# The third pair's decays and the last rows of batch 0 come by transfers instead of products, and the queue behind them is reordered

## The chip, the cores and the metric

The kernel runs on one core of a Trainium2 chip. The metric is the device time of one execution in microseconds (us), the median of several runs. Engines are named as in the profile: PE (matrix products), PEld (its weight loads), DVE (VectorE), ACT (ScalarE), POOL (GpSimd) and SP, whose queue issues nearly all transfers (DMAs).

## The reference

There are two stages. The first is a state space layer over 4 batches, 8 heads, 768 steps, 32 channels and 16 states, worked in chunks:

```python
log_a = np.log(np.clip(a, 1e-06, 1.0))
for c in range(nc):
    cum = np.cumsum(la, axis=-1)
    L = np.exp(cum[:, :, :, None] - cum[:, :, None, :]) * causal
    CB = np.einsum('bhin,bhjn->bhij', Cc, Bc)
    y_intra = np.einsum('bhij,bhjd->bhid', CB * L, xc)
    y_inter = np.einsum('bhin,bhnd->bhid', Cc, state) * decay_to_i[:, :, :, None]
    y[:, :, sl] = y_intra + y_inter
    state = decay_full[:, :, None, None] * state + np.sum(Bx, axis=2)
```

The second takes its output as 3072 tokens of 256 numbers through a layer of 2048:

```python
h = x @ w_in
g = h * (1.0 / (1.0 + np.exp(-1.702 * h)))
return (g @ w_out).astype(np.float32)
```

The two weights w_in and w_out are double precision in memory, and the kernel makes single precision of them itself.

## The kernel before

The tokens are worked in six groups of 512 (`g` = 0 to 5). A group has two *pairs* of chunks of 128 steps, so pair 0 and 1 belong to group 0, pair 2 and 3 (`PG` and `PG + 1`, here "the third and the fourth pair") to group 1. The change touches the stretch in which group 0 goes through both products while group 1's first stage is prepared, from about 22 to 82 us.

**The weights.** They come in ten pieces, 0 to 5 of w_in and 6 to 9 of w_out. `fetch(i)` issues two DMAs of a piece. `fields(i)` (L192, L195, on DVE) takes the words apart, `clamp(i)` (L203, L204, on ACT) bounds the exponent, `rounded(i)` (L208) adds the low word, and `join(i)` (L222, L228) writes the result into w_in or w_out; with `parts` 2 it does so in halves. `narrow(i)` does `rounded(i)`, `join(i)` and `fields(i + 1)`, and which of the last two comes first differs by piece. Raw words lie in four rotating buffers (`words`), which the spread decays share.

**Group 0's products.** `hidden(0, f)` for f = 0 to 15 makes one block h of the hidden layer by two products (L895), each a pair of records in the profile; ACT applies the nonlinearity (`silu`, L898). After them `project_all(0)` runs f = 0 to 15 again, with two products each into o0 and o1 (L992): f needs w_out's piece 6 + f / 4. Blocks h, the transposes `tp` and o0, o1 take turns in four PSUM banks.

**Group 1's preparation.** A pair's decay products within a chunk are a scan (`decay`, L405) over a, spread to all partitions; its end values scale B (`ends`, L464: Be). `spread(p)` brings the spread a by two DMAs of 256 KB from a scratch copy of a in DRAM, which `store_a` writes after a has been clipped. The third pair has another way: `pick_a` (ACT, L369) picks its rows, `fan_all` spreads them by products with ones (L415) into PSUM, and four scans (`decay_heads`, L453) follow. The decays since the start of a chunk (`since`) of batch 0's chunks 4 and 5 are likewise fanned out by products (L504, L533) and scanned in `since_fanned` (L546), while batch 1's come by one DMA (`spread_rows`, tile af), a clip (`clip_rows`, L483) and a scan (`decay_rows`, L496). `turn(p)` transposes B and C of a pair on PE (tp, L600), ACT copies them, and DVE multiplies C by `since` (CsT, L670). `score` (cb, L685), `gain` (A, L716), `keep_both`, `weigh` (L696) and `finish` (y, L825 and L839) complete the pair.

**What sets the order.** Every engine works in the order in which the program's lines are recorded; `in_order` keeps it. Dictionaries `in_hidden[0]` and `in_project[0]` say after which f of `hidden`, and before which f of `project_all`, a step is recorded:

```python
    at(in_hidden[0], 9, lambda: fan_all(PG))
    at(in_hidden[0], 9, since_fanned)
    at(in_project[0], 0, lambda: turn(PG), lambda: rounded(8),
       lambda: fields(9), lambda: join(8))
    at(in_project[0], 2, lambda: decay(PG + 1), lambda: clip_rows(1),
       lambda: decay_rows(1), lambda: turn(PG + 1))
    at(in_project[0], 9, lambda: score(pairs), lambda: gain(pairs), lambda: keep_both(pairs, True),
       lambda: weigh(PG), lambda: weigh(PG + 1))
    at(in_project[0], 15, lambda: finish(pairs))
```

From group 1 on the products take a form with seven instead of eight multiplications, for which DVE sums weights (`mix_in(n)`, L912: four sums for each of two blocks; `mix_w`) and values (`mix_y`, `mix_g`).

Of the kernel before, what the change touches and what calls it, by code (L numbers as in the profile page):

```python
# [16 lines left out]
P = 128  # L17
# [18 lines left out]
def kernel(  # L36
# [176 lines left out]
    NEXT = {1: (6,), 5: (9,)}  # L213
# [21 lines left out]
    def narrow(i):  # L235
        rounded(i)
        if i in (4, 5):
            join(i, 2)
        if i + 1 < len(PIECES):
            fields(i + 1)  # L240
        if i not in (4, 5):
            join(i)
# [23 lines left out]
    def spread_rows(b):  # L266
        raf[b] = raw.tile([P, NC, P], FP32, tag="af", name=f"af{b}", bufs=1)
        nc.sync.dma_start(out=raf[b].rearrange("p c s -> p (c s)"),
                          in_=a[b].unsqueeze(1).to_broadcast([NH, N, S]))

    def rows_a(t, queues):

        e = t.shape[1] * P
        for r in range(R):
            queues[r % len(queues)].dma_start(
                out=t[32 * r:32 * r + 32].rearrange("p c s -> p (c s)"),
                in_=a.rearrange("b h s -> (b h) s")[:, :e])
# [74 lines left out]
    starts, fans, flat = {}, {}, {}  # L352

    def clip(t, name):

        nc.vector.tensor_scalar(out=t, in0=t, scalar1=1e-6, scalar2=1.0,
                                op0=ALU.max, op1=ALU.min)
        starts[name] = const.tile([P, t.shape[1], 2], FP32, name=f"starts{name}")
        first = t.rearrange(by_chunk, s=2)[:, :, :, 0]
        nc.vector.tensor_copy(starts[name], first)  # L360
        nc.vector.memset(first, 0.0)

    def pick_a(p):

        b, c = divmod(2 * p, NC)
        X = ffn.tile([P, 2, DM], FP32, tag="ob", name=f"X{p}")
        X = fans[p] = X.rearrange("p k (q i) -> p k q i", q=Q)
        for q in range(Q):
            nc.scalar.activation(X[:, :, q], az[:, c:c + 2], AF.Copy, scale=pick[:, b, q:q + 1])  # L369

# [9 lines left out]
    pick = picker("pick", NB, 1, NH)  # L380
    whose = const.tile([32 * PG, 1 + PG, NH, N], FP32, name="whose")
    nc.gpsimd.memset(whose, 1.0)
    for i, n, head in ((0, 1, PG), (1, 2, PG), (0, 0, 1)):
        t = whose[32 * i:32 * i + 32, n:n + 1]
        nc.gpsimd.affine_select(out=t, in_=t, pattern=[[-1, 1], [-head, NH], [0, N]],
                                compare_op=ALU.is_equal, fill=0.0, base=-max(n - 1, 0),
                                channel_multiplier=1)
# [23 lines left out]
    def fan(p, r, ab):  # L411

        rows = slice(32 * r, 32 * r + 32)
        for i, side in enumerate(SIDES):
            nc.tensor.matmul(out=ab[side].rearrange("p (k q i) -> p k q i", k=2, q=Q),  # L415
                             lhsT=ones[rows, side], rhs=fans[p][rows][:, :, :, side],
                             start=True, stop=True, tile_position=(32 * r, H * i),
                             skip_group_check=True)

    def fan_all(p):  # L420

        ab = area(f"ab{p}")[:, :, :2 * Q * H]
        for r in range(R):
            fan(p, r, ab[:, r])
        fan_since()
        for r in range(R):
            decay_heads(p, r, ab[:, r])
        for k in range(2):
            ends(p, k)

# [15 lines left out]

    def decay_heads(p, r, ab):

        if r == 0:
            L = ssd.tile([P, R, 2 * Q * H], FP32, tag="L", name=f"L{p}", bufs=3)  # L450
            flat[p] = L
            Ls[p] = L.rearrange("p r (k q i) -> p k r q i", k=2, q=Q)
        nc.vector.tensor_tensor_scan(  # L453
            out=flat[p][:, r], data0=ab,
            data1=idents.rearrange("p h i -> p (h i)")[:, :2 * Q * H],
            initial=0.0, op0=ALU.mult, op1=ALU.add)
# [24 lines left out]
    def clip_rows(b):  # L481
        t = raf[b]
        nc.vector.tensor_scalar(out=t, in0=t, scalar1=1e-6, scalar2=1.0,  # L483
                                op0=ALU.max, op1=ALU.min)
        first = ssd.tile([P, NC, P], FP32, tag="first", name=f"first{b}", bufs=1)
        nc.gpsimd.memset(first, 0.0)
        f, t0 = (v.rearrange(by_chunk, s=2)[:, :, :, 0] for v in (first, t))
        nc.gpsimd.tensor_copy(f, t0)
        nc.gpsimd.memset(t0, 0.0)
        firsts[b] = first  # L490

    def decay_rows(b):

        t, first = raf.pop(b), firsts.pop(b)
        since[b] = ssd.tile([P, NC, P], FP32, tag="since", name=f"since{b}")
        nc.vector.tensor_tensor_scan(  # L496
            out=since[b].rearrange("p c s -> p (c s)"), data0=t.rearrange("p c s -> p (c s)"),
            data1=first.rearrange("p c s -> p (c s)"),
            initial=0.0, op0=ALU.mult, op1=ALU.add)

    def fan_rows(t, c0, c1, o):

        o = o[:, :(c1 - c0) * P]
        nc.tensor.matmul(out=o, lhsT=whose[:32, 0].rearrange("p h n -> p (h n)"),  # L504
                         rhs=t[:32, c0:c1].rearrange("p c s -> p (c s)"), start=True,
                         stop=True, tile_position=(0, 0), skip_group_check=True)
        return o

    def since_first():
# [3 lines left out]
        for p in range(PG):  # L513
            at = slice(32 * p, 32 * p + 32)
            nc.tensor.matmul(out=rows[p],
                             lhsT=whose[at, 1 + p].rearrange("p h n -> p (h n)"),
                             rhs=cum[at].rearrange("p k s -> p (k s)"), start=True, stop=True,
                             tile_position=(32 * p, 0), skip_group_check=True)
# [9 lines left out]

    def fan_since():
        o = bank("rows4")  # L530
        t = fanned["rows"] = fan_rows(az, CG, NC, o)
        f = fanned["starts"] = o[:, 2 * P:2 * P + 2 * (NC - CG)]
        nc.tensor.matmul(out=f, lhsT=whose[:32, 0].rearrange("p h n -> p (h n)"),  # L533
                         rhs=starts[1][:32, CG:].rearrange("p c s -> p (c s)"), start=True, stop=True,
                         tile_position=(0, 0), skip_group_check=True)

    fanned = {}

    def since_fanned():

        t, f = fanned["rows"], fanned["starts"]
        first = ssd.tile([P, NC, P], FP32, tag="first", name="first0", bufs=1)[:, CG:]
        nc.gpsimd.memset(first, 0.0)
        nc.vector.tensor_copy(first.rearrange(by_chunk, s=2)[:, :, :, 0],
                              f.rearrange("p (c s) -> p c s", s=2))
        nc.vector.tensor_tensor_scan(  # L546
            out=since[0][:, CG:].rearrange("p c s -> p (c s)"), data0=t,
            data1=first.rearrange("p c s -> p (c s)"), initial=0.0, op0=ALU.mult, op1=ALU.add)
# [340 lines left out]
    def hidden(g, f):  # L889
        j, i = divmod(f, 2)  # L890
        if i == 0:
            block(g, j)
        h = bank(f"h{g}_{f}")
        for k in range(NK):
            nc.tensor.matmul(out=h, lhsT=w_in[:, f, k], rhs=yT[g][:, k], start=(k == 0),  # L895
                             stop=(k == NK - 1), skip_group_check=True)

        nc.scalar.activation(gT[g, j][:, i], h, AF.Silu, scale=GELU_SCALE)  # L898
# [303 lines left out]
    rows_a(az, (nc.sync,))  # L1202
# [14 lines left out]
    load(PG)  # L1217
# [7 lines left out]
    def store_a():  # L1225
        clip(az, 1)
        for i, side in enumerate(SIDES):
            nc.sync.dma_start(out=scratch[:, i].rearrange("c r i -> r c i"), in_=az[:32, :, side])

    at(in_hidden[0], 5, store_a, lambda: fetch(7), lambda: fetch(8),  # L1230
       lambda: load(PG + 1))
    at(in_hidden[0], 8, lambda: pick_a(PG))
    at(in_hidden[0], 9, lambda: fan_all(PG))
    at(in_hidden[0], 9, since_fanned)
    for i, k, c in ((2, 1, 1), (3, 2, 2), (4, 4, 7), (5, 8, 11), (6, 11, 14), (7, 14, 15)):
        at(in_hidden[0], k, lambda i=i: narrow(i))
        at(in_hidden[0], c, lambda i=i: clamp(i + 1))
    at(in_hidden[0], 9, lambda: spread(PG + 1), lambda: spread_rows(1))
# [5 lines left out]
    at(in_project[0], 2, lambda: decay(PG + 1), lambda: clip_rows(1),  # L1244
       lambda: decay_rows(1), lambda: turn(PG + 1))
    at(in_project[0], 5, lambda: narrow(9))
    at(in_project[0], 9, lambda: score(pairs), lambda: gain(pairs), lambda: keep_both(pairs, True),
# [3 lines left out]
       lambda: load(n + 1, "x"), lambda: mix_in(2), lambda: mix_in(3),  # L1251
       lambda: turn_blocks(2), lambda: decay(n))
# [10 lines left out]
    at(after, "H1", lambda: turn_out(0, 0), lambda: turn_out(0, 1))  # L1263
# [62 lines left out]
    for j in range(2):  # L1326
        mix_g(1, j)
    run(1, "4.1 4.5 4.2 P P 4.6 P L P 4.7 P P P 4.D", seven(1, 0), L=more_loads)
# [121 lines left out]
```

## Time and profile before

| what | us |
|---|---|
| median of 3 runs | 349.3 (348.98 to 349.34) |
| profiled execution | 350.67 |
| its span, first to last instruction | 348.8 |
| PE busy | 341.6 |
| DVE busy | 254.6 |
| ACT busy | 155.0 |

The clock granted to PE was 1.0 throughout. The chain of work that ended last is PE for 90% of the span, DMA for 3%, DVE for 2%. A row of a timeline gives start, duration, engine, line, operation, tiles (out<-in) and, in brackets, the idle time of the engine before it and what ended it; rows of the chain give start, duration and what ran. Rows of SP are issues: their duration is the time that the queue took to accept them, not that of the transfer.

### The profile page before, as it was taken

How to read it: one execution, taken by the hardware profiler on the slowest of the kernel's cores; microseconds unless marked ns; L12 is line 12 of the kernel's file. 1: busy time of each engine (PE TensorE's matmuls, PEld its weight loads, DVE VectorE, ACT ScalarE, POOL GpSimd, SP SyncE). 2: the span in 40 equal slices, each digit the busy share in tenths (PEclk: the TensorE clock that was granted, in tenths of full speed). 3: DMA queues.
4: the chain of work that ended last, by engine and by line, in shares of the span. 5: the costliest groups of instructions: out<-in, count | busy, mean ns of one | idle time of the engine just before them, and what ended most of it. 6: DMA issues, size and time to landing. Idle time of an engine off the chain costs nothing.

```text
span 348.8 us, 8124 instructions
## 1 busy us (share of the span) xinstructions
PE 341.6 (98%) x3380; PEld 268.9 (77%) x3380; DVE 254.6 (73%) x481; ACT 155.0 (44%) x352; POOL 13.1 (4%) x42
## 2 busy tenths in 40 slices
PE   8989999999999999999999999999999999999996
PEld 6634444445688888888888888888888888899996
DVE  5889997999878999667997467788465654465463
ACT  4797585205453322654432554332564331554320
POOL 8300000100000100000000000000000000000000
PEclk9999999999999999999999999999999999999999
DMA  6599889624627200415704027400000300000301
GB/s 158 134 300 213 189 181 245 113 54 105 113 49 131 66 0 2 75 57 124 123 18 63 0 59 130 73 1 2 0 4 3 55 7 0 0 2 0 62 0 61
DMA packets 89980, 25.92 MB, mean 74 GB/s; under 512 B 73432, under 2 KB 87128, under 8 KB 89944
## 3 DMA queue, kind: packets, MB, share of 16 engines
q1 hardware_dynamic: 89112, 24.88, 33.5%
q10 hardware_dynamic: 832, 0.52, 0.5%
q8 instruction: 26, 0.43, 0.5%
q14 instruction: 10, 0.08, 0.1%
HBM read 22.15 MB, written 3.24 MB: 73 GB/s over the span
## 4 chain that ended last, share of the span: by engine, by line
PE 90%; DMA 3%; DVE 2%; SPq 1%; ACT 1%; issue 1%; ACTq 1%; POOL 0%; DVEq 0%
PE acc L1055 28%; PE X L950 19%; PE Y L960 14%; PE o L992 8%; PE acc L1062 7%; PE h L895 5%; DMA bits<-in_moe_w_in_dram 3%; PE y L839 2%; PE cb L685 2%; PE y L825 1%; SPq L180 1%; PE A L716 1%; PE ab L557 1%; DMA zC<-in_C_dram 1%; DVE p L222 1%
## 5 line engine op out<-in xcount | busy, mean ns | idle before, releaser
L955 ACT ACTIVATE ac<-X 128x256 f32<-128x256 f32 x76 | 29.1, 383 | 81.5 <-PE X L950 80.7
L1082 DVE TENSOR_TENSOR gT<-Y,ac 128x512 f32<-128x512 f32 x38 | 26.2, 689 | 40.1 <-PE Y L960 32.5
L1055 PE MATMUL acc<-mg,mw 128*128 128x256 f32 x192 | 54.5, 379 | 0.0
L927 ACT ACTIVATE gT<-gT 128x512 f32<-128x512 f32 (+1 forms) x76 | 38.9, 518 | 29.0 <-DVE gT L1082 28.5
L950 PE MATMUL X<-my,mi 128*128 128x256 f32 x152 | 45.1, 380 | 0.0
L1055 PEld LDWEIGHTS acc<-mg,mw 128*128 128x128 f32 x192 | 36.5, 190 | 5.0
L895 PE MATMUL h<-yT,w_in 128*128 128x512 f32 x80 | 35.6, 598 | 1.1 <-DVE w_in L228 0.6
L1082 DVE TENSOR_TENSOR gT<-Y,b 128x256 f32<-128x256 f32 x38 | 15.9, 419 | 28.5 <-PE Y L960 28.5
L1055 PE MATMUL acc<-gT,w_out 128*128 128x256 f32 x128 | 35.5, 379 | 0.0
L950 PEld LDWEIGHTS X<-my,mi 128*128 128x128 f32 x152 | 28.0, 190 | 3.9 <-ACT ac L955 0.2
L895 PEld LDWEIGHTS h<-yT,w_in 128*128 128x128 f32 x80 | 14.7, 190 | 19.7 <-issue 15.9
L992 PE MATMUL o<-gT,w_out 128*128 128x512 f32 x64 | 28.3, 595 | 0.0
L918 DVE TENSOR_TENSOR mg<-gT 128x512 f32<-128x512 f32 x40 | 27.2, 681 | 0.0
L1055 PEld LDWEIGHTS acc<-gT,w_out 128*128 128x128 f32 x128 | 24.2, 190 | 3.4 <-ACT yT L873 0.2
L955 ACT ACTIVATE b<-X 128x256 f32<-128x256 f32 x38 | 14.6, 383 | 21.2 <-PE X L950 20.7
L950 PE MATMUL X<-yT,w_in 128*128 128x256 f32 x76 | 23.2, 389 | 0.0
L960 PE MATMUL Y<-yT,w_in 128*128 128x256 f32 x76 | 22.7, 381 | 0.0
L960 PE MATMUL Y<-my,mi 128*128 128x256 f32 x76 | 22.7, 380 | 0.0
L960 PE MATMUL Y<-yT,mi 128*128 128x256 f32 x76 | 22.5, 379 | 0.0
L950 PE MATMUL X<-my,w_in 128*128 128x256 f32 x76 | 22.5, 379 | 0.0
L992 PEld LDWEIGHTS o<-gT,w_out 128*128 128x128 f32 x64 | 11.8, 190 | 13.6 <-issue 13.4
L405 DVE TENSOR_TENSOR_SCAN L<-a,idents 128x1024 f32<-128x1024 f32 x9 | 20.5, 2277 | 0.2 <-DMA a<-scratch 0.2
(159 smaller groups left out, 546.9 us busy)
## 6 DMA issues: line engine op xcount, KB each, us to landing
a<-scratch SPq DMA_DIRECT2D x18, 256.0 KB, 4.8
bits<-in_moe_w_out_dram SPq DMA_DIRECT2D x8, 512.0 KB, 6.6
x<-in_x_dram SPq DMA_DIRECT2D x24, 128.0 KB, 3.1
out_dram<-ob SPq DMA_DIRECT2D x40, 64.0 KB, 1.9
bits<-in_moe_w_in_dram SPq DMA_DIRECT2D x8, 256.0 KB, 4.4
bits<-in_moe_w_in_dram SPq DMA_DIRECT2D x4, 512.0 KB, 11.9
b<-in_B_dram SPq DMA_DIRECT2D x20, 64.0 KB, 2.6
af<-in_a_dram SPq DMA_DIRECT2D x3, 384.0 KB
```

The costliest lines, as they stand in the source:

```text
L405: nc.vector.tensor_tensor_scan(out=L, data0=ra[p].rearrange("p k e -> p (k e)"), data1=idents.rearrange("p h i -> p (h i)"), initial=0.0, ...
L685: nc.tensor.matmul(out=s["cb"][side, r, k].rearrange("p (q i) -> p q i", q=Q), lhsT=BT[rows, k, side], rhs=CT[rows, k, :, side], start=Tru ...
L895: nc.tensor.matmul(out=h, lhsT=w_in[:, f, k], rhs=yT[g][:, k], start=(k == 0), stop=(k == NK - 1), skip_group_check=True)
L918: nc.vector.tensor_tensor(out=t[:, 0:2], in0=B[:, :, 1], in1=B[:, 0], op=ALU.subtract)
L927: nc.scalar.activation(o, i, AF.Silu, scale=GELU_SCALE)
L950: nc.tensor.matmul(out=s["X"], lhsT=lhsT, rhs=rhs, start=i == "1", stop=i == "4", skip_group_check=True)
L955: nc.scalar.activation(copy, s["X"], AF.Copy)
L960: nc.tensor.matmul(out=o, lhsT=lhsT, rhs=rhs, start=s.pop("new", False), stop=i != "5", skip_group_check=True)
L992: nc.tensor.matmul(out=o[c], lhsT=w_out[:, c, f], rhs=gT[g, f // 2][:, f % 2], start=(f == 0), stop=(f == NF - 1), skip_group_check=True)
L1055: nc.tensor.matmul(out=acc[g][0][i][:, cols], lhsT=w, rhs=h[:, cols], start=(j == 0 and k == 0 and (i, 0) in begins), stop=(j == NF // 2 - ...
L1062: nc.tensor.matmul(out=o[k] if type(o) is list else o[:, cols], lhsT=h[:, cols], rhs=w, start=(j == 0 and (i, k) in begins), stop=(j == NF ...
L1082: nc.vector.tensor_tensor(out=o, in0=v, in1=w, op=ALU.add)
```

## The change

- The third pair's a comes by `spread(PG)` and one scan of 1024 (`decay(PG)`, after f = 15 of hidden), as the fourth's does; `pick_a`, `fan`, `fan_all`, `decay_heads` and the picker that they use are gone.
- Batch 0's chunks 4 and 5 come by `spread_rows(0)`, 128 KB, with `clip_rows(0)` at f = 11 and `decay_rows(0)` ahead of piece 7's join; `fan_rows`, `fan_since` and `since_fanned` are gone. a itself is loaded once and not four times.
- The order of the queue: behind the scratch writes now come piece 7, the third pair's x, piece 8, batch 0's rows, piece 9, the fourth pair's B and C, the third pair's spread, the fourth pair's x, batch 1's rows, the fourth pair's spread. Before it was the third pair's x, the scratch writes, pieces 7 and 8, the fourth pair's B, C and x, piece 9, the fourth pair's spread, batch 1's rows.
- `narrow` joins ahead of the next fields for pieces 2 and 6 too, and piece 3 is joined in halves. Piece 5 to 7's clamps and joins are placed otherwise.
- The products h of f = 10 to 14 are done in two halves of 256 columns.
- The scores and gains stand ahead of f = 10 of project_all, not 9. `mix_in(2)` and `mix_in(3)` are recorded later, after group 0's `turn_out` and after group 1's second `mix_g`.

```diff
-    NEXT = {1: (6,), 5: (9,)}
+    NEXT = {1: (6,)}
 ...
     def narrow(i):
         rounded(i)
-        if i in (4, 5):
-            join(i, 2)
+        if i in (2, 4, 5, 6):
+            join(i, 2 if i in (4, 5) else 1)
         if i + 1 < len(PIECES):
             fields(i + 1)
-        if i not in (4, 5):
-            join(i)
+        if i not in (2, 4, 5, 6):
+            if i == 7:
+                decay_rows(0)
+            join(i, 2 if i == 3 else 1)
 ...
     def spread_rows(b):
-        raf[b] = raw.tile([P, NC, P], FP32, tag="af", name=f"af{b}", bufs=1)
+        c = CG if b == 0 else 0
+        raf[b] = raw.tile([P, NC, P], FP32, tag="af", name=f"af{b}", bufs=1)[:, c:]
 ...
+        n = 2 if g == 0 and f in range(10, 15) else 1
         for k in range(NK):
-            nc.tensor.matmul(out=h, lhsT=w_in[:, f, k], rhs=yT[g][:, k], start=(k == 0),
-                             stop=(k == NK - 1), skip_group_check=True)
+            for i in range(n):
+                cols = slice(i * TG // n, (i + 1) * TG // n)
+                nc.tensor.matmul(out=h[:, cols], lhsT=w_in[:, f, k], rhs=yT[g][:, k, cols],
+                                 start=(k == 0 and i == 0), stop=(k == NK - 1),
+                                 skip_group_check=True)
 ...
-    load(PG)
+    load(PG, "bc")
 ...
-    at(in_hidden[0], 5, store_a, lambda: fetch(7), lambda: fetch(8),
-       lambda: load(PG + 1))
-    at(in_hidden[0], 8, lambda: pick_a(PG))
-    at(in_hidden[0], 9, lambda: fan_all(PG))
-    at(in_hidden[0], 9, since_fanned)
-    for i, k, c in ((2, 1, 1), (3, 2, 2), (4, 4, 7), (5, 8, 11), (6, 11, 14), (7, 14, 15)):
+    at(in_hidden[0], 5, store_a, lambda: fetch(7), lambda: load(PG, "x"), lambda: fetch(8),
+       lambda: spread_rows(0))
+    at(in_hidden[0], 11, lambda: clip_rows(0))
+    for i, k, c in ((2, 1, 1), (3, 2, 2), (4, 4, 7), (5, 8, 9), (6, 9, 13), (7, 13, 15)):
         at(in_hidden[0], k, lambda i=i: narrow(i))
         at(in_hidden[0], c, lambda i=i: clamp(i + 1))
-    at(in_hidden[0], 9, lambda: spread(PG + 1), lambda: spread_rows(1))
+    at(in_hidden[0], 9, lambda: fetch(9), lambda: load(PG + 1, "bc"), lambda: spread(PG),
+       lambda: load(PG + 1, "x"), lambda: spread_rows(1), lambda: spread(PG + 1))
+    at(in_hidden[0], 15, lambda: decay(PG))
 ...
-    at(in_project[0], 2, lambda: decay(PG + 1), lambda: clip_rows(1),
+    at(in_project[0], 2, lambda: clip_rows(1), lambda: decay(PG + 1),
        lambda: decay_rows(1), lambda: turn(PG + 1))
     at(in_project[0], 5, lambda: narrow(9))
-    at(in_project[0], 9, lambda: score(pairs), lambda: gain(pairs), lambda: keep_both(pairs, True),
+    at(in_project[0], 10, lambda: score(pairs), lambda: gain(pairs), lambda: keep_both(pairs, True),
        lambda: weigh(PG), lambda: weigh(PG + 1))
     at(in_project[0], 13, lambda: mix_in(1), lambda: spread(n + 1, held=True),
-       lambda: load(n + 1, "x"), lambda: mix_in(2), lambda: mix_in(3),
-       lambda: turn_blocks(2), lambda: decay(n))
+       lambda: load(n + 1, "x"), lambda: turn_blocks(2), lambda: decay(n))
 ...
-    at(after, "H1", lambda: turn_out(0, 0), lambda: turn_out(0, 1))
+    at(after, "H1", lambda: turn_out(0, 0), lambda: turn_out(0, 1), lambda: mix_in(2))
 ...
     for j in range(2):
         mix_g(1, j)
+    mix_in(3)
```

## The prediction

> **What bounds the kernel now.** I read the page first, then the chain of waits between 34 and 82 us, then the timelines of VectorE (DVE) and of the DMA queue (SP) there. All times are us from the span's start. On the page PE is busy 98% of the span and 90% of the chain of waits is PE, so only PE's standstills and PE work that goes away can bring time.
>
> ```profile
> PE 341.6 (98%) x3380; PEld 268.9 (77%) x3380; DVE 254.6 (73%) x481; ACT 155.0 (44%) x352; POOL 13.1 (4%) x42
> ```
>
> The chain shows where PE runs and what it stands for. Before 39.02 come ACT's picking of a, then the fan products; after it PE runs without a gap, but for 0.5 us at 67 (the products L716 wait for CsT).
>
> ```profile
> 36.74 0.80 ACT X L369 x2
> 37.54 0.04 issue
> 37.59 0.69 PE ab L415 x16
> 38.28 0.62 PE rows L504 x2
> 38.91 0.12 PE rows L533 x2
> 39.02 10.50 PE h L895 x24
> ...
> 53.39 0.44 PE tp L600 x4
> 53.83 12.02 PE o L992 x28
> 65.85 1.15 PE cb L685 x63
> ...
> 67.53 0.78 PE A L716 x44
> 68.30 10.50 PE o L992 x24
> 78.80 0.97 PE y L825 x56
> ```
>
> So one f of h, or of o, costs PE 10.50 / 6 = 1.75 (12.02 / 7 = 1.72). The next rows are VectorE's: the only one of its waits that is long is for the last piece of w_out, at 57.72; the scan of the fourth pair's decays stands at 61.32, the CsT for which PE waits at 67.04.
>
> ```profile
> 57.72 0.69 DVE L192 TENSOR_SCALAR p<-bits 128x1024 uint32<-128x1024 uint32 x1 [1.77 <-DMA bits<-in_moe_w_out_dram]
> 61.32 2.28 DVE L405 TENSOR_TENSOR_SCAN L<-a,idents 128x1024 f32<-128x1024 f32 x1
> 67.04 0.42 DVE L670 TENSOR_TENSOR CsT<-tp,since 128x256 f32<-128x256 f32 x1
> ```
>
> The queue: it is one line in order, and it is full. An issue of b takes 0.5 at 65 us, but here 2.2 to 2.6 each, while the four pieces ahead drain.
>
> ```profile
> 38.51 2.12 SPq L180 DMA_DIRECT2D bits<-in_moe_w_out_dram  x4
> 40.67 4.82 SPq L150 DMA_DIRECT2D b<-in_B_dram  x2
> 45.53 3.01 SPq L150 DMA_DIRECT2D c<-in_C_dram  x2
> ```
>
> **Part by part: what goes off PE.** The sixteen ab records and four of rows (0.69 + 0.62 + 0.12) and the wait for ACT's X (0.84) go: f9 ended at 36.5, f10 began at 39.0, so 2.5. Piece 2's join now comes ahead of the next piece's fields, which waited 0.75 for their DMA: its w_in is written at 25.1, not 26.0, so f4 starts at 25.26 and not 26.18 (0.9). Piece 3 gives half of that back: fields(4) still start at 26.87, when the DMA has landed, and f6 waits for its half-join until about 29.1 instead of the due 28.7 (0.4). Together f10 starts at 36.0, 3.0 sooner.
>
> **What comes back on ACT.** clamp(6) moves ahead of the silus of f10 and f11, clamp(7) ahead of f14's. A clamp is two instructions of 1.15. fields(6) finish their first half at 39.9, clamp(6) ends at 42.3, f10's silu at 42.9, and f14, which takes its PSUM bank, waits 0.1. join(6) follows clamp(6) to 44.8, fields(7) to 45.4, clamp(7) to 47.8, f14's silu to 48.35: the second half of o f0 takes that bank, was due at 47.7, and waits 0.7. What is left: the second turn (tp L600 of the fourth pair) due at 51.1, against 53.39: 2.3 sooner.
>
> **Edits at nothing.** The h of f10 to f14 in halves: 128x256 records run at 0.86 for four in the chain, 0.215 each, half of a 512 one; even. POOL loses one picker and one select (about 2), but the second CT there waited for VectorE's L652 anyway. clip of a is as long on 32 rows as on 128 by its row length (0.55); its copy of starts (0.17) goes. mix_in(2) and mix_in(3) (four sums, 1.47 each) leave VectorE's stretch at 76 to 79 and go before two gT sums (L1082) that stood idle 2.17 and 1.74: hidden there. Without that cover each would cost PE up to 1.5.
>
> **What moves in the queue.** Three of four a copies go, x of the third pair steps behind piece 7, and VectorE's memset of a, on which the scratch writes wait, is done at 35.4 (before at 35.3; piece 3's join in four instructions costs 0.3, the copy of starts is saved): scratch is issued there instead of at 37.37, behind x, and piece 7 2.0 sooner. But then x (two issues), piece 8, the rows of a (128 KB), and piece 9 (two issues) all stand ahead of the fourth pair's b and c, where only pieces 7 and 8 did. The four issues of 7 and 8 land 5.4 to 7.9 after their issue, from 43.9 to 48.0: 1.4 apiece. x takes about 0.9 an issue (L150's own two are issued 0.6 apart and land 1.0 apart), the rows 0.4 (a third of 384 KB). c landed, by the b ahead at 48.95 and the x behind at 51.5, at about 50.3. Now: 50.3 - 2.0 + 1.7 + 2.8 + 0.4 = 53.2; I take 53.5, since c's own issues are held up behind more small packets. Bounds 52.0 (the tail of 7 and 9 drains at once) and 54.3. PE waits at the second turn from 51.1 to 53.5: o f2 starts at 54.05, where before it was 53.83. **The gain of PE's first stage is gone here.** Behind the turn on PE stand all products of w_out.
>
> **What the transfer costs that replaces the fan.** The third pair's spread (two issues of 256 KB) stands behind c. c's second issue ends 1.8 ahead of its landing, so the spread's are issued at about 51.8 and 52.4. Where the queue was otherwise idle, at 76.5 and 103.7, a spread landed 4.0 to 4.8 after its issue. 52.4 + 4.7 = 57.1. Bounds: 53.5 plus the 1.69 and 1.32 by which the spread's halves followed piece 9 (57.6, 59.3, 60.6), 56.5, from below, or 55.0 with c at 52.0; from above the spread of before, which had the same two pieces, b, c and x ahead of it and landed at 60.6: 60.6 - 2.0 + 0.4 = 59.0. I take the idle rows, as little is queued behind.
>
> The Trainium skill, "DMA: Bandwidth & Descriptors", section "Anatomy of one DMA — SWDGE (gpsimd) path", puts a transfer at about 2.0 us fixed plus its bytes over 436 GB/s; that is stated for the other issue path. An estimate by it is 3.2 for these 512 KB, which would end the sum 1.5 sooner, at 349.1; the two idle rows (4.0 to 4.8) do not agree with it.
>
> VectorE does the scan at the end of piece 7's join, 54.1 (the clip of a's rows waits for them until about 48), so it stands from 54.1 to 57.1, and behind it on VectorE stand join(8), which PE's f8 needs, and the fourth pair's CsT, which A needs. Then, each by its pitch in the timeline: scan 2.33, Be 0.41, CsT 0.34, rounded(8) 1.14, fields(9) 1.21, join(8) 2.39, clip of rows 0.60, the fourth pair's scan 2.32, Be 0.41, since 1.76, CsT 0.40: 13.3. CsT ends at 70.4 and A starts at 70.55. On PE alone A would be due at f2 + 8 x 1.72 + 1.15 = 68.95, so VectorE decides. join(8) is done at 64.9 for f8, due at 64.4: 0.5, inside that wait. From A to y: 0.78 + 5 x 1.75 = 9.5 (five f, not six, since the scores stand one place later): y starts at 80.1, not 78.80. **1.3 later.** In short: shift of y = the larger of (spread lands - 55.8) and (c lands - 53.8).
>
> Behind y nothing gains or loses: VectorE had ended weigh 3.9 ahead of y, and has 2.9 us less to do after 76.4; PE's next stages have no wait in the view. So the span goes from 348.8 to 350.1. The profiled execution took 350.67, 1.4 above the median 349.3 of the unprofiled runs; 1.3 more is 352.0 for the one and 350.6 for the other. A measurement of this kernel can tell about 0.2%, 0.7 us, from no change.
>
> **Rivals.** (1) *Faster:* the queue drains without its tail, c lands by 52.5 and the spread by 55.0. For it: 512 KB land every 1.4, and the engines show a DMA share under 0.8 at 46 to 50, so room is left. Against: b's issues took over 2 us each, and piece 9 landed 6.9 after its issue. The shift is -0.8 at 55.0, at best -2.0: 348.5 to 347.3. It decides from 55.1 on. 0.18. (2) *No change:* the spread follows c as it did piece 9, or quicker, and lands between 55.1 and 56.5; the gain and the two waits cancel: 348.6 to 350.0. For it the 1.69 and 1.32; against it both idle rows. The page named above would put it here. 0.20. (3) *Slower still:* the spread lands like that of before, at 59, as the fourth pair's x, rows and spread read beside it: shift 3.2, 352.5. For it the 8.0 to 8.6 from issue to landing at 51 to 60; against it that those were issued behind piece 9 directly. 0.20. The forecast, 56.5 to 58.2: 0.42.
>
> **How the numbers follow.** Faster by over 0.2% is rival 1, 0.18; within it, rival 2, 0.20; slower, the forecast and rival 3, 0.62. The range from 348.2 to 352.5 leaves out the better half of rival 1 and the worse part of rival 3. The forecast's own range is 350.0 to 351.7.
>
> **What would show it.** In the profile after: no ab or rows L504 between f9 and f10, and f10 at 36.0; PE waiting at tp for a DMA of c, to about 53.5; VectorE waiting at the scan L for a<-scratch, to about 57; A waiting for CsT until about 70.5; y at about 80. If tp has no wait over 1 us and the scan none, the queue was misjudged and rival 1 holds; if PE's first stage gains under 2, the first part was wrong.

## The result and the profile after

| | before | after |
|---|---|---|
| median of five runs each on one chip, us | 349.34 (348.98 to 350.17) | 354.62 (354.36 to 355.46) |
| ratio, 95% interval | | 1.016 (1.015 to 1.018) |
| profiled execution, us | 350.67 | 355.46 |
| its span, us | 348.8 | 353.3 |

The kernel after is slower by 5.3 us. In the two profiled executions it is 4.55 of span. 2.1 of this have come up when the first products y of group 1 start (80.83 against 78.73), and 2.45 come behind them (272.5 from y to the end, against 270.0). The granted clock of the five executions of after is between 0.994 and 1.0; the last section says what that costs. Two rows of PE's timeline of before, the first turn and the first y of group 1:

```profile
49.36 0.38 PE L600 MATMUL tp<-ident,b 128*128 128x128 f32 x2
...
78.73 1.04 PE L825 MATMUL y<-CsT,S 32*64 32x64 f32 x56
```

The page of after, first PE's line: PE has as much work as before in a longer span, and only 71% of the chain (90% before); DVE has 13% and DMA 6%.

```profile
PE 341.6 (97%) x3380; PEld 271.8 (77%) x3380; DVE 254.3 (72%) x479; ACT 154.1 (44%) x350; POOL 15.3 (4%) x38
```

PE's timeline of after, 45 to 84 us; in brackets the time for which PE stood, and what ended that. It goes from h to the transposes at 45.95, where before did so at 49.36. Then it stands 2.2 at the second turn (three waits, for b and c), 1.73 for piece 8 and 0.36 for CsT.

```profile
45.95 0.38 PE L528 MATMUL tp<-ident,b 128*128 128x128 f32 x2
...
47.68 2.84 PE L925 MATMUL o<-gT,w_out 128*128 128x512 f32 x6 [0.27 <-ACT gT L831]
51.71 0.50 PE L528 MATMUL tp<-ident,b 128*128 128x128 f32 x2 [1.19 <-DMA b<-in_B_dram]
52.98 0.33 PE L528 MATMUL tp<-ident,c 128*128 128x128 f32 x1 [0.77 <-DMA c<-in_C_dram]
53.56 0.33 PE L528 MATMUL tp<-ident,c 128*128 128x128 f32 x1 [0.25 <-DMA c<-in_C_dram]
53.73 10.46 PE L925 MATMUL o<-gT,w_out 128*128 128x512 f32 x24
65.92 3.70 PE L925 MATMUL o<-gT,w_out 128*128 128x512 f32 x8 [1.73 <-DVE w_out L228]
...
71.34 0.78 PE L644 MATMUL A<-x,Be 64*32 64x64 f32 x54 [0.36 <-DVE CsT L598]
...
80.83 1.04 PE L753 MATMUL y<-CsT,S 32*64 32x64 f32 x56
```

VectorE's timeline of after shows why piece 8 and CsT are late: it stands 2.3 for the rows of a and 4.7 for the third pair's spread, and has no gap from there to CsT.

```profile
47.70 0.29 DVE L439 TENSOR_SCALAR af<-af 128x256 f32<-128x256 f32 x1 [2.32 <-DMA af<-in_a_dram]
57.98 2.29 DVE L392 TENSOR_TENSOR_SCAN L<-a,idents 128x1024 f32<-128x1024 f32 x1 [4.67 <-DMA a<-scratch]
70.86 0.42 DVE L598 TENSOR_TENSOR CsT<-tp,since 128x256 f32<-128x256 f32 x1
```

The queue's timeline of after: piece 9 is now ahead of b and c; the two issues of b take 4.21 together, the two of c 3.22, and the spread follows at 51.50.

```profile
42.96 0.93 SPq L180 DMA_DIRECT2D bits<-in_moe_w_out_dram  x2
43.93 4.21 SPq L150 DMA_DIRECT2D b<-in_B_dram  x2
48.18 3.22 SPq L150 DMA_DIRECT2D c<-in_C_dram  x2
51.50 1.31 SPq L261 DMA_DIRECT2D a<-scratch  x2
```

All this the prediction had described, in kind if not in size. What it had not is 30 us later. VectorE's timelines around 103 to 114, two lines of before and two of after: the memset that lets the spread of p be issued, and the scan that reads that spread.

```profile
103.62 0.06 DVE L256 MEMSET a<- 128x1 f32 x1
...
109.27 2.29 DVE L405 TENSOR_TENSOR_SCAN L<-a,idents 128x1024 f32<-128x1024 f32 x1 [0.17 <-DMA a<-scratch]
```

```profile
107.45 0.06 DVE L258 MEMSET a<- 128x1 f32 x1
...
113.82 2.29 DVE L392 TENSOR_TENSOR_SCAN L<-a,idents 128x1024 f32<-128x1024 f32 x1 [2.36 <-DMA a<-scratch]
```

In after mix_in(3), which the change moved, stands directly ahead of the memset (105.95 to 107.5). The scan was 0.17 from its transfer before, and is 2.36 from it now. Behind it wait Be, a sum of gT, ACT and then PE:

```profile
117.75 0.70 PE L883 MATMUL X<-my,mi 128*128 128x256 f32 x2 [1.36 <-ACT ac L888]
```

### The profile page after: what moved, and what is told of

Read it like the earlier page. It is cut to its first block, busy times and chain, and to the rows that moved or that the text cites. A ratio compares the mean times of both kernels' runs of the same rounds, so it can differ in the third digit from the quotient of the medians.

```text
span 353.3 us, 8114 instructions
## 1 busy us (share of the span) xinstructions
PE 341.6 (97%) x3380; PEld 271.8 (77%) x3380; DVE 254.3 (72%) x479; ACT 154.1 (44%) x350; POOL 15.3 (4%) x38
## 4 chain that ended last, share of the span: by engine, by line
PE 71%; DVE 13%; DMA 6%; SPq 5%; issue 2%; ACT 1%; DVEq 0%
PE acc L988 25%; PE X L883 18%; PE Y L893 13%; PE acc L995 7%; DMA a<-scratch 3%; DVE p L222 2%; DVE L L392 2%; PE y L767 2%; PE cb L613 2%; SPq L180 2%; DMA af<-in_a_dram 2%; PE y L753 1%; SPq L150 1%; DMA x<-in_x_dram 1%; PE o L925 1%
## 5 line engine op out<-in xcount | busy, mean ns | idle before, releaser
L826 PE MATMUL h<-yT,w_in 128*128 128x512 f32 (+1 forms) x100 | 35.1, 509 | 0.5 <-ACT yT L786 0.5
L826 PEld LDWEIGHTS h<-yT,w_in 128*128 128x128 f32 x100 | 18.8, 190 | 15.3 <-issue 11.2
L392 DVE TENSOR_TENSOR_SCAN L<-a,idents 128x1024 f32<-128x1024 f32 x10 | 22.8, 2280 | 8.7 <-DMA a<-scratch 8.7
```

The lines of the kernel that those rows point to most:

```text
L392: nc.vector.tensor_tensor_scan(out=L, data0=ra[p].rearrange("p k e -> p (k e)"), data1=idents.rearrange("p h i -> p (h i)"), initial=0.0, ...
L826: nc.tensor.matmul(out=h[:, cols], lhsT=w_in[:, f, k], rhs=yT[g][:, k, cols], start=(k == 0 and i == 0), stop=(k == NK - 1), skip_group_ch ...
```

## The experiments

Theory A after this reading: two losses that have little to do with one another. The first is in the queue between 34 and 66 us, the second is the place of the memset. Each kernel below was timed in five rounds beside the kernel before on the same chip. Kernels of different rounds are compared by their medians; the kernel before itself took 348.96 to 349.37 in these rounds, so differences below 0.4 between them say nothing. "From y to the end" is the span less the start of group 1's first y in the profiled execution: 270.0 before, 272.5 after.

### The late loss: e3, e8, e1, e5

**e3** is the kernel before with only mix_in(2) and mix_in(3) moved as in the change.

```diff
-       lambda: load(n + 1, "x"), lambda: mix_in(2), lambda: mix_in(3),
-       lambda: turn_blocks(2), lambda: decay(n))
+       lambda: load(n + 1, "x"), lambda: turn_blocks(2), lambda: decay(n))
-    at(after, "H1", lambda: turn_out(0, 0), lambda: turn_out(0, 1))
+    at(after, "H1", lambda: turn_out(0, 0), lambda: turn_out(0, 1), lambda: mix_in(2))
     for j in range(2):
         mix_g(1, j)
+    mix_in(3)
```

> The kernel before with nothing changed but the place of mix_in(2) and mix_in(3), which go where the kernel after has them. Theory A (the memset behind mix_in(3)): the memset of a and the spread of p come about 1.5 later, the scan of p waits about 1.5 where it waited 0.17, and PE loses about 1.0 to 1.5: 350.3 to 350.8, from 349.3. Rival (the prediction's own step, that the two are hidden there and nothing behind y moves): 349.3 within 0.4.

Measured: 351.28 against 349.37, ratio 1.004 (1.003 to 1.006), and 271.9 from y to the end. The rest of the change is not in this kernel, and from y to the end it has 1.9 of the 2.45 that after has. VectorE's timeline of e3, then PE's line behind it:

```profile
103.86 0.06 DVE L256 MEMSET a<- 128x1 f32 x1
...
109.85 2.29 DVE L405 TENSOR_TENSOR_SCAN L<-a,idents 128x1024 f32<-128x1024 f32 x1 [1.99 <-DMA a<-scratch]
```

```profile
113.78 0.70 PE L950 MATMUL X<-my,mi 128*128 128x256 f32 x2 [0.97 <-ACT ac L955]
```

It lost 1.9, a little over what theory A gave it; the rival, the prediction's own step, falls.

**e8** is e3 with that memset and its two issues recorded ahead of the sums of values.

```diff
+    spread(p, held=True)
     for j in range(2):
         mix_g(1, j)
     mix_in(3)
 ...
     def more_loads():
-        spread(p, held=True)
```

> The kernel before with mix_in(2) and mix_in(3) moved as in the change, which alone made it 1.9 us slower, and with the memset of a for p recorded ahead of the two mix_g and of mix_in(3). Theory A: all of the 1.9 is the place of the memset, so it is back at the time before: 349.3 within 0.4. Rival B: it is VectorE's 1.5 us for mix_in(3) in a stretch that has no room: 350.5 or more.

Measured: 348.86 against 348.96, ratio 1.000 (0.999 to 1.001), 270.0 from y to the end. In VectorE's timeline of e8 the scan has no wait, with mix_in(3) in the same place:

```profile
98.39 0.06 DVE L256 MEMSET a<- 128x1 f32 x1
...
106.82 2.28 DVE L405 TENSOR_TENSOR_SCAN L<-a,idents 128x1024 f32<-128x1024 f32 x1
```

So the sums' own 1.5 us of VectorE are indeed hidden there, as the prediction said; the 0.06 us instruction behind them was not.

**e1** puts the two mix_in of the kernel after back where they stood (the diff of e3 the other way).

> The kernel after with mix_in(2) and mix_in(3) back where they stood before (ahead of turn_blocks(2) and decay(n)), all else as after. Theory A: of the 4.5 us that the span grew, about 2.2 are lost late because the memset that lets the spread of p go stands behind mix_in(3) on VectorE. With mix_in(3) back the memset comes some 1.5 sooner, the scan of p waits 0.2 to 1.0 instead of 2.36, ACT's ac is not late, and the late 2.2 go; but VectorE's 2.9 us are ahead of decay(n) again, with y already 2.0 late, so the next pair's A waits about 1.3. Sum: 354.6 - 2.2 + 1.3 = 353.7, between 352.4 and 354.2. Rival B: the late loss only follows from y being late, whatever stands ahead of the memset: then nothing is won and the wait ahead of decay(n) comes on top, 354.6 to 355.9.

Measured: 354.78, ratio 1.013 (1.009 to 1.017): no gain in the median, which lies in rival B's range. But the trace shows both halves of theory A: the wait at the scan of p is 0.80 instead of 2.36 and PE's waits for ac are 0.3 in all, and PE waits 1.14 for Be at the next pair's A, 3 us of sums being ahead of that pair's decays again. From y to the end it takes 271.9, 0.6 less than after. Its profiled execution also has two stretches at half clock, and its executions without one took 353.1 and 354.0, within theory A's range (last section), so the time alone decides nothing here.

**e5** is the kernel after with the memset and its two issues moved as in e8.

> The kernel after with spread(p, held=True), that is the memset of a on VectorE and the two issues behind it, recorded ahead of the two mix_g and of mix_in(3) instead of behind them; mix_in(3) stays where the change put it. Theory A (the late loss is the place of the memset, not the sums' own time): the memset comes 4.5 us sooner, the spread lands before the scan of p is due, the wait of 2.36 there goes, and with it the late 1.9 that the kernel before lost to the same move: 354.6 - 1.9 = 352.7, between 352.2 and 353.5. Rival B (VectorE has no room for mix_in(3) there, wherever the memset stands): PE still waits for ACT's ac, and the time stays over 354.

Measured: 353.15, ratio 1.010 (1.009 to 1.012), 1.5 less than after by the medians (1.1 less, if each is counted from the kernel before beside it); 270.1 from y to the end, with no wait at the scan of p. The memset stands at 104.55 there, and the scan at 112.98. Theory A holds, rival B falls.

### The first loss: e2, e9, e12, e4

**e2** moves piece 9 behind b, c and the third pair's spread.

```diff
-    at(in_hidden[0], 9, lambda: fetch(9), lambda: load(PG + 1, "bc"), lambda: spread(PG),
+    at(in_hidden[0], 9, lambda: load(PG + 1, "bc"), lambda: spread(PG), lambda: fetch(9),
```

> The kernel after with the fourth pair's b and c and the third pair's spread queued ahead of piece 9 of w_out instead of behind it. Theory A: piece 9 (two issues at 1.4 apiece) delays c and the spread by about 2.8. Without it c lands near 50.7, PE does not wait at the second turn, the spread lands near 54.3, A starts near 67.8 and y near 77.3 to 78, and all of that goes through: 354.6 - 3 = 351.4, between 350.5 and 352.2. Piece 9 lands later by 2 to 3 and is needed for f8 only. Rival: c and the spread are slow by their own small packets, not by piece 9: they land within 0.7 of where they do now, 354 to 354.6.

Measured: 354.51, ratio 1.014 (1.009 to 1.018). The first half of theory A came: no wait at the second turn (50.39), A at 67.83. But y starts at 80.24, not 77.3 to 78. The time is the rival's, its reason is not: c and the spread did land sooner. VectorE's timeline of e2:

```profile
55.13 2.29 DVE L392 TENSOR_TENSOR_SCAN L<-a,idents 128x1024 f32<-128x1024 f32 x1 [1.22 <-DMA a<-scratch]
65.65 2.29 DVE L392 TENSOR_TENSOR_SCAN L<-a,idents 128x1024 f32<-128x1024 f32 x1 [1.66 <-DMA a<-scratch]
70.27 0.42 DVE L598 TENSOR_TENSOR CsT<-tp,since 128x256 f32<-128x256 f32 x1
```

The third pair's scan starts 2.85 sooner than in after; then the fourth pair's stands for its own spread, CsT ends 0.6 sooner, and A waits 2.62 for it. In after that second spread was hidden behind the first.

**e9** is the kernel after without the third pair's spread; a constant stands in its place, so the output is not that of the reference.

```diff
+        if p == PG:
+            nc.gpsimd.memset(ra[p], 0.5)
+            return
```

> The kernel after without the third pair's spread: GpSimd fills that tile with a constant instead (so the third pair's decays are not those of the input). It tells what the transfer that replaces the fan costs, apart from the rest of the queue. Theory A (VectorE's stand at that scan sets y): c lands as in the kernel after, at 53 to 53.5, VectorE does not stand at the scan of the third pair, f8 and A do not wait, and y starts at 78.0 to 79.0 instead of 80.8; what stands behind the spread in the queue comes 2 to 3 sooner. 354.6 - 2.3 = 352.3, between 351.5 and 353.0. Rival B (the queue as a whole): the stand only moves to the rows or the fourth pair's spread, y is at 80 or later and the time over 353.5.

Measured: 352.69, ratio 1.012 (1.008 to 1.016); y at 78.46, 2.4 sooner than in after, with the second turn still waiting 2.3 for b and c; 272.4 from y to the end, so the late loss is untouched. The time is within theory A's range. Its interval overlaps that of after (1.015 to 1.018), so the gain rests on the trace: of the first loss, 2.4 is the transfer that took the fan's place, with what it held up in the queue behind it.

**e12** takes the third pair's x back ahead of the writes to scratch.

```diff
-    load(PG, "bc")
+    load(PG)
-    at(in_hidden[0], 5, store_a, lambda: fetch(7), lambda: load(PG, "x"), lambda: fetch(8),
+    at(in_hidden[0], 5, store_a, lambda: fetch(7), lambda: fetch(8),
```

> The kernel after with only the third pair's x back ahead of the writes to scratch. The prediction's step says that the change gained there (scratch issued 2.0 sooner): then undoing it costs up to 1, 354.6 to 355.6. Theory A (full engines from 36 us on, and scratch waits for VectorE's clip at about 34.5 wherever x stands): c and the spread land about 1.5 sooner, y is at 79 to 79.6, 353.2, between 352.6 and 353.8.

Measured: 353.07, ratio 1.011 (1.008 to 1.013), y at 78.25. Undoing that move wins 1.5 (1.3, counted from the kernel before beside each), which is theory A; the prediction's step falls. Scratch is issued at 34.8 in both kernels, as VectorE's clip ends then. There x is issued from 32.1 to 33.8; in after the queue issues nothing from 32.9 to 34.8.

**e4** is the kernel before with only piece 2's join ahead of the fields and piece 3's in halves.

```diff
-        if i in (4, 5):
-            join(i, 2)
+        if i in (2, 4, 5):
+            join(i, 2 if i > 2 else 1)
 ...
-        if i not in (4, 5):
-            join(i)
+        if i not in (2, 4, 5):
+            join(i, 2 if i == 3 else 1)
```

> The kernel before with nothing changed but piece 2's join ahead of the next piece's fields and piece 3's join in two halves. Theory: f4 starts 0.9 sooner, f6 waits 0.4, so PE's first stage ends 0.5 sooner, and the second turn is not late for the queue, as c lands 2.5 ahead of it: 348.8, from 349.3. Rival: the wait is met again at ACT's picking of a (X), which is VectorE's clip and not moved by it: 349.3 within 0.2.

Measured: 350.60, ratio 1.004 (1.001 to 1.006): no gain, and outside both ranges. The forty records of h before f10 take 17.43 in e4 and the same 17.43 in e3, which has the old order of joins: the 0.75 for which VectorE waited for piece 3 in the profiled execution of before (f4 0.9 late) is not in e3's. PE's wait for X is 1.46 in e4 and 0.75 in e3. About half of the 0.4% is stretches at half clock, which five of its twelve executions had (last section); whether the longer wait for X is the rest, no run shows.

### Putting it right: e6, e7, e10, e11

**e6** queues in the order of need.

```diff
-    at(in_hidden[0], 5, store_a, lambda: fetch(7), lambda: load(PG, "x"), lambda: fetch(8),
-       lambda: spread_rows(0))
+    at(in_hidden[0], 5, store_a, lambda: fetch(7), lambda: spread_rows(0),
+       lambda: fetch(8))
-    at(in_hidden[0], 9, lambda: fetch(9), lambda: load(PG + 1, "bc"), lambda: spread(PG),
-       lambda: load(PG + 1, "x"), lambda: spread_rows(1), lambda: spread(PG + 1))
+    at(in_hidden[0], 9, lambda: load(PG + 1, "bc"), lambda: spread(PG), lambda: fetch(9),
+       lambda: spread_rows(1), lambda: spread(PG + 1), lambda: load(PG, "x"),
+       lambda: load(PG + 1, "x"))
```

> The kernel after with the queue in the order in which the first stage needs it: the rows of a ahead of piece 8, the fourth pair's b and c and the third pair's spread ahead of piece 9, the fourth pair's rows and spread ahead of both x. Theory A (the first loss is the order of the queue alone): VectorE's waits of 2.32, 4.67 and, in the kernel with only the third pair's spread moved, 1.66 shrink under 1 each, PE has no wait at the second turn, A is due by PE at about 66.5 and y starts at 75.5 to 77.5 instead of 80.8; from y on as after: 354.6 - 4 = 350.6, between 349.9 and 351.5. Rival B (the queue's whole load: 512 KB more in 20 us than before, whatever the order): what gains for one spread is lost for the next or for x, y is at 79.5 or later and the time over 353.

Measured: 354.47, ratio 1.015 (1.012 to 1.018). Neither side was right as put, though the time and the reason are rival B's: y is at 78.00, 2.8 sooner, and then PE gives it back at the next pair, whose spread comes late. PE's timeline of e6:

```profile
88.68 0.52 PE L644 MATMUL A<-x,Be 64*32 64x64 f32 x24 [2.47 <-DVE Be L420]
```

The engines are full: in the stretches of 3 us their mean busy share is 1.0 or over from 51 to 63 us in e6, and one issue of the fourth pair's x takes from 55.7 to 62.6.

**e7** is e6 with the early memset of p, and the one of pair n + 1 ahead of mix_in(1).

> Both of these together, and the memset of the second next pair's a ahead of mix_in(1) as well. Theory A (two losses that have nothing to do with one another, so they add): 354.6 - 4 - 1.9 - 0.3 = 348.4, between 347.6 and 349.6: no slower than the kernel before, at best 0.5% faster. Rival B (the gains overlap, as PE's end is set by one chain): not under 350.

Measured: 351.31, ratio 1.008 (1.006 to 1.011), y at 77.19. Rival B is right: 2.35 of the 5.3 are left against the kernel before beside it, so it wins 2.9 and not theory A's sum of 6.2. Part of the rest is a wait of 1.55 for Be at the next pair, and what follows on it (last section).

**e10** is e7 with x back as in e12.

> The kernel with the queue in the order of need and both memsets early, and with the third pair's x back where the kernel before had it, ahead of the writes to scratch, when the queue stood idle from 32.9 to 34.8. Theory A (the engines are full from 36 to 63 us, and each transfer moved into that stretch costs its own time there): 1.8 less of it, so the spreads land 1 to 2 sooner, VectorE stands under 1.2 at the third pair's scan and not at all at the second next pair's, y is at 76 or sooner. 351.3 - 2 = 349.3, between 348.3 and 350.3. Rival B (x is read out of cover, its place is the same to all): 351 to 351.6.

Measured: 351.24, ratio 1.006 (1.003 to 1.009): the median of e7, rival B. VectorE still stands 2.78 for the third pair's spread. The 1.5 that x won in e12 is not won again where piece 9 stands behind the spread; why, no run here takes apart.

**e11** is e10 with the third pair's spread issued by ACT, on its own queue.

```diff
+    at(in_hidden[0], 9, lambda: spread(PG, queue=nc.scalar))
-    at(in_hidden[0], 9, lambda: load(PG + 1, "bc"), lambda: spread(PG), lambda: fetch(9),
+    at(in_hidden[0], 9, lambda: load(PG + 1, "bc"), lambda: fetch(9),
```

> The same, with the third pair's spread issued by ACT on its own queue at about 37.5, as soon as scratch has landed, instead of by SP behind c at 46. Theory A (bandwidth, not the line of issues, is what lacks): the spread lands before 49, but piece 8 and c come 1 to 2 later, and the time is within 0.8 of the kernel that has it on SP. Rival B (the line of issues lacks): VectorE does not stand, c lands as before, y is 1 sooner or more, and the time under 348.5, faster than the kernel before.

Measured: 351.47, ratio 1.006 (1.004 to 1.008). The spread, issued at 38.6, lands at 49.15 and VectorE does not stand for it; piece 8 lands so much later that VectorE stands 4.11 for that, and PE 1.9 for b and c. Theory A: the bytes lack room, not the issues. The Trainium skill says so ("DMA: Bandwidth & Descriptors", section "Issuing engines are not separate DMA queues"): what different engines issue runs on the same 16 DMA engines and interleaves there, and only the time to issue is saved. The trace agrees.

No kernel of these beats the kernel before; e8, the moved sums with the early memset, equals it.

## Why the prediction was wrong

The direction was right and the size was not: 350.6 and at most 352.5 were forecast, 354.62 came. Two steps failed.

**"Behind y nothing gains or loses".** The prediction listed mix_in(2) and mix_in(3) among the edits at nothing, "hidden there", and looked for the two sums' duration only. It did not list what is recorded behind mix_in(3) on VectorE: a memset of 0.06, on which two issues on SP wait, on which a scan waits that had 0.17 to spare. The line of before that says it, the scan at 109.27, was not read. e3 shows its price alone (1.9), e8 and e5 that it goes away with the memset's place.

**"1.3 more is 352.0 for the one and 350.6 for the other".** The 1.3 was counted from y in the profiled execution, which was itself 1.33 over the median, and was then put on the median as well. But y starts at 78.73 in that execution and at 77.44 in e3, whose first stage is the same:

```profile
77.44 1.04 PE L825 MATMUL y<-CsT,S 32*64 32x64 f32 x56
```

So the first stage lost about 3.4 against an execution without that lateness (80.83 less 77.44; by the medians 5.3 less 1.9), not the 2.1 that the traces of before and after show. Two of the gains that the prediction listed were in part this lateness. The wait ahead of f4 (0.9) is not in e3; it did not count in the end, as the second turn took PE's whole gain. Scratch, issued at 37.37, was 2.0 behind the end of VectorE's memset; with the same old order it is issued 1.3 behind it in e3 (35.81) and 0.9 in e8 (34.42), so of the 2.0 that was taken off for c and the spread only about half was the order's.

Added up: 1.9 behind y, 1.3 for the late y that was counted from, and 0.7 by which y came later than forecast (80.83 for 80.1) are 3.9 of the 4.0 missed. That it closes so well is in part luck, as three of the five executions of after are not like the profiled one (last section).

**What held.** f10 was at 35.60 (forecast 36.0) and the second turn due at 50.5 (51.1). Against e3 PE's first stage gained 2.3 and not 3.0 (f10 started 17.27 after the first h in after, 35.60 less 18.33, and 19.55 in e3). The fan and the wait for X are nearly all of it: their terms in the prediction add up to 2.27, not to the 2.5 that it wrote. o f2 started at 53.73 (54.05): as said, the gain of PE's first stage was gone there, for b and c behind piece 9; e2 and e6, where these stand ahead of it, have no wait. VectorE stood for the spread, for 4.67 and not 3.0: it was free 0.8 sooner (53.3 for 54.1), and the spread landed 0.8 later (57.9 for 57.1), within its bounds of 55.0 and 59.0. Only the landing counts for y; that term was 0.8 short, and it went through nearly whole (CsT at 70.86, A at 71.34 for 70.55, y at 80.83 for 80.1). The wait for join(8) at f8 was 1.73, not 0.5, but then A waited 0.36 where the forecast had 1.1 left for it: both waits end by the same chain on VectorE. e9 gives the spread 2.4 in all, against after.

The rule "shift of y = the larger of (spread lands - 55.8) and (c lands - 53.8)" is 2.1 by 57.9, as measured against the profiled execution. It is incomplete, as e2 shows: with the third pair's spread and c early, the fourth pair's spread sets y.

**The rivals.** "Faster" and "no change" both needed the spread to land by 56.5, and it did not. "Slower still" was nearest in its time, but its one mechanism, the spread at 59, did not come. The 3.2 that the prediction worked out by the Trainium skill ("DMA: Bandwidth & Descriptors", section "Anatomy of one DMA — SWDGE (gpsimd) path") did not come either: in after the spread took 5.7 from its second issue (52.2 to 57.9).

## What to carry to other kernels

Before calling a moved step hidden, look at the next instructions that its engine has to do behind it, the shortest ones above all: a memset that only lets a transfer go carries the slack of whatever reads that transfer, and that slack stands in the profile as the reader's wait. Moving work from products to transfers needs room on the transfer engines in that very stretch; here they were full, and a better order of the queue mostly moved the wait to the next reader (e2, e6). And when the profiled execution is slower than the median, find the waits that only it has before taking them off as gains.

## What the runs showed of the hardware

A standstill of PE had a second price in some executions. In e7 PE waited 1.55 for Be from 85.5 to 87.0; the rows of 1 us there show the granted clock (PEclk, the third number from the right) at 0.50 from about 89 to 92, though PE was busy again:

```profile
85.00:86.00 1.00, 0.48 (x33) 0.31 (x32) 1.00 (x1) 0.60 (x1) 0.00 (x0) 1.00 0.25 66
86.00:87.00 1.00, 0.00 (x0) 0.00 (x0) 0.97 (x3) 0.00 (x0) 0.00 (x0) 1.00 0.24 68
...
89.00:90.00 1.00, 1.00 (x2) 0.34 (x1) 0.86 (x5) 0.31 (x2) 0.00 (x0) 0.50 0.67 65
90.00:91.00 1.00, 1.00 (x2) 0.34 (x1) 0.85 (x3) 0.00 (x0) 0.00 (x0) 0.50 0.07 5
91.00:92.00 1.00, 1.00 (x2) 0.34 (x1) 0.87 (x3) 0.00 (x0) 0.00 (x0) 0.50 0.87 94
```

Eight records of h took 5.40 there instead of 3.70, so 1.7 were lost beside the 1.55. e6 (after a wait of 2.47) and e1 (after the waits at its second turn) show the same, while after's own profiled execution, with 2.2 of waits at the second turn, does not.

Added up from such rows (one at 0.90 holds 0.2 us at half clock), the slow stretch lasts 3.4 us in e7, in e6 and both times in e1 (11.6 to 15.0 and 56.0 to 59.4), and 6.8, twice that, in e5 (17.8 to 24.6, after a wait of 1.89). Half of 3.4 is 0.5% of these spans: a mean clock of 0.995 on record fits one such stretch, 0.990 two. In the kernel before, 62 of the 63 executions beside the experiments have 0.999 or over. In after three of five had one stretch (354.36 to 354.62) and two had none (355.33 and 355.46), so the 5.3 us are not the clock's; what those three waited less, no trace here shows. In e4 five of twelve had one or two (351.65 to 353.79), and the other seven have a median of 350.02. In e10 four of twelve had (352.76 to 354.13), and the other eight have a median of 350.5.

The Trainium skill ("TensorE: Matmul & The Clock Gate", Part 1, "The HAM clock gate") puts the clock at half after at least one idle window of about 3.4 us, the window running freely. The length of the slow stretch, 3.4 or twice that, agrees. That 1.55 us of standstill was enough does not; that it happens in some executions and not in others is what a window that runs freely would make, but no view here shows where its windows begin.
